# Two chunks of sequence 0 first, sequence 1's input transform spread over both, and the first weight sums split between VectorE and GpSimd

## The chip, the cores and the metric

The kernel runs on one core of one Trainium2 chip. The metric is the device time of the whole launch in microseconds. Engines are named as the profile names them: PE (matmul) with its weight loader PEld, DVE (VectorE), ACT (ScalarE), POOL (GpSimd), and SP, which here only issues DMAs. Matmul results go to PSUM, which the kernel uses as eight banks of 512 fp32 columns; everything else lies in SBUF.

## The reference

A convolution of width 3 along the sequence with 1024 input and 1024 output channels, then a batch norm from stored statistics and a SiLU:

```python
xp = jnp.pad(x, ((0, 0), (1, 1), (0, 0)))            # x: (2, 2048, 1024) bf16
y = sum(einsum('bsc,cd->bsd', xp[:, k:k + S], w[k]) for k in range(3))   # w: (3, 1024, 1024)
y = (y - mean) * (g / sqrt(var + 1e-5)) + b
return silu(y)
```

## The kernel before

**The algorithm.** The convolution is done with short polynomial products: six neighbouring output positions need eight products of transformed inputs with transformed weights, where the direct form needs eighteen. A sequence of 2048 has `NB` = 342 blocks of six positions. The input transform turns each block into eight values (`NJ` = 8) per channel, kept in SBUF as `T_sb` for both sequences. The weight transform makes, for each chunk of 128 output channels, six combinations of w0, w1, w2 (products 1 to 6); products 0 and 7 use w0 and w2 as they are.

**The input transform** (`t_jobs`, `t_job`). Rows of x are loaded in 17 overlapping windows per sequence: sixteen of up to 128 rows in the buffers `xw` (12 of them) and the first window in `xfirst`. A window is multiplied on PE by a small constant matrix, four channel tiles at a time (4 matmuls of 168 columns into two PSUM banks), and the result is copied from PSUM to `T_sb` by ACT or DVE (lines 276 and 278). I call four such matmuls with their copy a group; there are 33 groups per sequence, numbered here 0 to 32 for sequence 0 and 33 to 65 for sequence 1. A small planner with an estimated clock per engine (`clock`, `ends`, `busy`) decides, when the program is written, which of ACT and DVE copies a group. Nothing is reordered at run time: each engine works through its own list in the order written, and a PE instruction whose PSUM bank is still being copied holds up every PE instruction behind it.

**A unit** (`Unit`) is one chunk of 128 output channels (`dc`, 0 to 7) for one sequence (`bi`): eight products of 8 matmuls of 342 columns each, line 311. It owns four banks, the next unit the other four. `run` issues products 1, 3, 2, 4, 5, 6 with ACT copies of some results (`copy`, lines 322 and 324) and DVE combinations (`combine`, line 329) between them. Products 7 and 0 of a unit (`last`, `first`) and its SiLU passes (`silu_inner`, line 334) are issued during the next unit, at the places given by `place`. Product 6 is added onto product 5's bank, so it waits until ACT has copied product 5 (`pc`).

**The order before.** All 33 groups of sequence 0 run first, then 15 groups of sequence 1 (`ahead`, without products), then unit (0,0) with the last 18 groups between its matmuls (`Between`, about one group per 2.6 matmuls, in bank pairs from 4, 6 and, in the first four products, 1), and then units (0,1), (1,0), (1,1), (2,0) and so on. In unit (0,0), which has no earlier unit's products to put between its products 5 and 6, four extra calls of `between` stand there.

**The weights.** The sums of chunk 0 (`prepare_first`, written behind group 18) run on POOL: sum e0 = w0 + w2 (line 174), its two combinations u0 (line 194), and the same for e1 and e2, which need w2 and w0 times four and w1 times two. ACT makes two of these three multiples (lines 162 and 180), POOL one (line 183). Later chunks (`prepare_w`) are made two at a time, e1 and e2 as one DVE instruction each (line 176), the rest on POOL. Chunk 1 is made during unit (0,0) and the one after it.

**The loads.** SP issues them in one list: sequence 0's windows, with the three weight loads of chunk 0 behind windows number 4, 6 and 8 of the order (`W0_AT`); then sequence 1's windows, with chunk 1's weights behind numbers 5, 8 and 11 (`W1_AT`). The weights of chunks 2 and 3 follow after unit (0,0), into memory that the windows had.

Of the kernel before, what the change touches and what calls it, by code (L numbers as in the profile page):

```python
# [9 lines left out]
ALU = mybir.AluOpType  # L10
# [5 lines left out]
P = 128  # L16
R = 6
NJ = 8
W0_AT = (4, 6, 8)
W0_USE = 18  # L20
W1_AT = (5, 8, 11)
AMONG = 18
XBUFS = 12
# [3 lines left out]
def kernel(  # L27
# [24 lines left out]
    epool = ctx.enter_context(tc.tile_pool(name="epool", bufs=1))  # L52
    spool = ctx.enter_context(tc.tile_pool(name="spool", bufs=2))
    ypool = ctx.enter_context(tc.tile_pool(name="ypool", bufs=1))
    dpool = ctx.enter_context(tc.tile_pool(name="dpool", bufs=1))
# [102 lines left out]

    def double_w(dc, eng):
        t = spool.tile([P, CT, P], BF16, name="w1x2")  # L160
        if eng is nc.scalar:
            nc.scalar.mul(t, raw[dc][:, 1], 2.0)  # L162
            busy("act", CT * P)
        else:
            eng.tensor_scalar(t, raw[dc][:, 1], 2.0, 0.0, op0=ALU.mult, op1=ALU.add)
        double[dc] = t

    def even_part(dc, q, eng, by=None):

        w0, w2 = raw[dc][:, 0], raw[dc][:, 2]  # L170
        e = epool.tile([P, CT, P], FP32, name=f"e{q}")
        f, h = (w2, w0) if q == 1 else (w0, w2)
        if q == 0:
            eng.tensor_tensor(e, w0, w2, op=ALU.add)  # L174
        elif eng is nc.vector:
            eng.scalar_tensor_tensor(out=e, in0=f, scalar=4.0, in1=h, op0=ALU.mult, op1=ALU.add)  # L176
        else:
            t = spool.tile([P, CT, P], BF16, name="w1x2")
            if by is nc.scalar:
                by.mul(t, f, 4.0)  # L180
                busy("act", CT * P)
            else:
                by.tensor_scalar(t, f, 4.0, 0.0, op0=ALU.mult, op1=ALU.add)
            eng.tensor_tensor(e, t, h, op=ALU.add)
        if eng is nc.vector:
            busy("dve", CT * P)
        sums[dc, q] = e

    def transform_w(dc, q):

        o = double[dc] if q else raw[dc][:, 1]
        u = upool.tile([P, 2, CT, P], BF16, name=f"u{q}")
        for i, op in enumerate((ALU.add, ALU.subtract)):
            nc.gpsimd.tensor_tensor(u[:, i], sums[dc, q], o, op=op)  # L194
        wts[dc, q] = u

    def prepare_w(dc):

        even_part(dc, 0, nc.gpsimd)
        transform_w(dc, 0)  # L200

        def second():
            even_part(dc, 1, nc.vector)
            transform_w(dc, 1)

        def third():
            even_part(dc, 2, nc.vector)
            transform_w(dc, 2)

        act_work.append(lambda: double_w(dc, nc.scalar))  # L210
        dve_work.extend((second, third))

    def prepare_first(dc):

        even_part(dc, 0, nc.gpsimd)
        transform_w(dc, 0)
        double_w(dc, nc.scalar)
        for q, eng in ((1, nc.scalar), (2, nc.gpsimd)):
            even_part(dc, q, nc.gpsimd, eng)
            transform_w(dc, q)  # L220

# [65 lines left out]
    class Unit:  # L287
# [8 lines left out]

        def __init__(self, dc, bi, b0, lo=0, hi=NB):
            self.dc, self.bi, self.b0, self.lo, self.hi = dc, bi, b0, lo, hi
            self.bank = [ps[:, b0 + q, lo:hi] for q in range(4)]
            self.low, self.mid, self.high = (ps[:, b0 + q:b0 + q + 2, lo:hi] for q in range(3))  # L300
            self.yT = yts[bi]

# [48 lines left out]

        def run(self, between, prev, place=(5, 6), prepare=None):


            finish = {n: [] for n in range(4, 7)}
            if prev:
                finish[min(place[0], 5)].append(prev.silu_inner)
                finish[place[0]].append(lambda: prev.last(between))
                finish[place[1]].append(lambda: prev.first(between))

            def behind(n):
                for f in finish[n]:
                    f()

# [6 lines left out]
            self.product(3, 1, False, between)  # L371
            pa = self.copy(3)
            self.product(0, 3, False, between)
            pb = self.copy(0, by=4.0)
            self.product(3, 2, True, between)
            self.copy(3, dst=sd[:, 0])
            self.combine(sd[:, 1], pa, 2.0, b3, ALU.subtract)
            self.product(0, 4, True, between)
            behind(4)
# [7 lines left out]
            pc = self.copy(2)  # L387
            if not prev:
                for _ in range(4):
                    between()  # L390
            behind(5)
# [65 lines left out]
    def ahead(jobs, job_n):  # L457
        for job in jobs:
            t_job(job, job_n % 4 * 2)
            if job_n == 0:  # L460
                params()
            if job_n == 4:
                scales()
            if job_n == W0_USE:
                prepare_first(0)
            job_n += 1

    jobs0 = list(t_jobs(0))
    ahead(jobs0, 0)
    for i, wi in enumerate(order):  # L470
        load_x(1, wi)
        if i in W1_AT:
            load_w(0, W1_AT.index(i), 1)
    jobs1 = list(t_jobs(1))
    ahead(jobs1[:-AMONG], len(jobs0))

    class Between:

        n = done = 0
        jobs = jobs1[-AMONG:]  # L480

        def __call__(self):
            self.n += 1
            while self.jobs and self.done * 46 < self.n * AMONG:
                t_job(self.jobs.pop(0), (4, 6, 1)[self.done % (3 if self.n <= 4 * CT else 2)])
                self.done += 1

    between = Between()
    seq = [(dc, bi) for dc in range(DC) for bi in range(B)]
    before = prev = None  # L490
    for i, (dc, bi) in enumerate(seq[:-1]):
        unit = Unit(dc, bi, i % 2 * 4)
        unit.run(
            between, prev, (4, 4) if i >= len(seq) - 3 else (5, 6),
            1 if i == 0 else 2 if i == 2 else dc + 2 if bi == 1 and 0 < dc < DC - 2 else None,
        )
        if i == 0:
            while between.jobs:
                between()
            xwin_scope.close()  # L500
            olast = ctx.enter_context(tc.tile_pool(name="olast", bufs=2))
            wpools[1] = ctx.enter_context(tc.tile_pool(name="wpool1", bufs=1))
        if i in (0, 4, 8):
            for k in range(3):
                load_w(i // 4 + 1, k)
# [6 lines left out]
        before, prev = prev, unit  # L512
    dc, bi = seq[-1]
    h0 = Unit(dc, bi, 4, P, NB)
    h0.run(between, prev, (5, 5))
    prev.turn(olast)
    h1 = Unit(dc, bi, 0, 0, P)
    h1.run(between, h0, (5, 6))
    o = olast.tile([P, R, NK, P], BF16, name="o")
# [37 lines left out]
```

## Time and profile before

| what | value |
|---|---|
| runs | 196.32 us median of 3 (194.3 to 197.12) |
| the profiled execution | 195.83 us; span from first to last instruction 194.1 us |
| granted PE clock | 0.985 of full speed on average, 1.0 until 185 us |
| busy in the span | PE 176.8 us (91%), DVE 157.9, POOL 135.9, ACT 110.3 |
| first group / first product matmul starts | 3.90 us / 27.66 us |
| last group's matmuls start | 39.02 us to 39.84 us |

Times inside the execution count from the start of the span. A busy share is the part of a stretch in which an engine had an instruction running. A line of the timeline gives the start, the length, the engine, the line of the kernel and the tiles; in square brackets is the idle time ahead of it and what ended it. "x2" is two instructions merged into one line.

### The profile page before, as it was taken

Reading aid. Unit: us, or ns where it says so; the run is one execution under the profiler, and the core shown is the slowest. Engines: PE = TensorE matmul, PEld = TensorE weight load, DVE = VectorE, ACT = ScalarE, POOL = GpSimd, SP = SyncE. Lnnn points to the kernel's source line nnn. Section 1 sums busy time; section 2 is a strip of 40 time slices with the busy share of each in tenths; the row PEclk is TensorE's granted clock in tenths of the full one; section 3 lists DMA queues with packets and bytes.
Section 4 is the critical chain, followed back from the end, with each engine's and each line's share of the span. In section 5 each row is a group of like instructions: output and inputs, shape, how many; then the busy total and the mean of one; then the engine's idle time right before and its main releaser. Section 6 shows DMA issues by size and latency. Waiting matters only on the chain.

```text
span 194.1 us, 3673 instructions
## 1 busy us (share of the span) xinstructions
PE 176.8 (91%) x1379; PEld 125.4 (65%) x1379; DVE 157.9 (81%) x221; ACT 110.3 (57%) x185; POOL 135.9 (70%) x76
## 2 busy tenths in 40 slices
PE   1888879999999999999999999999999998989940
PEld 0876658766666666666666666666666665668920
DVE  5579866689978799988998899899889994747940
ACT  3589876774546556455546562737383572636630
POOL 5569999906796889999999999799997760000000
PEclk9999999999999999999999999999999999999985
DMA  5999998074142837597869659959649295773685
GB/s 189 310 334 306 347 330 267 8 222 107 30 91 53 179 73 159 163 217 179 163 96 202 115 117 272 209 115 193 123 111 201 50 194 99 158 156 67 151 180 120
DMA packets 89115, 32.30 MB, mean 166 GB/s; under 512 B 75721, under 2 KB 84937, under 8 KB 89097
## 3 DMA queue, kind: packets, MB, share of 16 engines
q1 hardware_dynamic: 87784, 31.75, 70.6%
q10 hardware_dynamic: 1313, 0.31, 0.7%
q8 instruction: 11, 0.18, 0.4%
q14 instruction: 7, 0.06, 0.1%
HBM read 14.82 MB, written 8.39 MB: 120 GB/s over the span
## 4 chain that ended last, share of the span: by engine, by line
PE 79%; DMA 8%; ACT 4%; DVE 2%; SPq 1%; issue 1%; ACTq 1%; DVEq 0%
PE ps L311 74%; DMA xw<-in_x_dram 6%; PE ps L265 5%; ACT yT L334 2%; DMA rows<-in_b_dram 2%; SPq L130 1%; ACT T_sb L276 1%; DVE ps L329 1%; ACTq L71 1%; ACT w1x L162 0%; ACT pc L322 0%; DVE T_sb L278 0%; DVE t L329 0%; SPq L146 0%; DVE o L413 0%
## 5 line engine op out<-in xcount | busy, mean ns | idle before, releaser
L311 PE MATMUL ps<-T_sb,u 128*128 128x342 bf16 (+2 forms) x816 | 119.8, 299 | 1.4 <-ACT pc L322 1.2
L311 PEld LDWEIGHTS <-u 128*128 128x128 bf16 x816 | 76.8, 97 | 35.3 <-issue 2.1
L194 POOL TENSOR_TENSOR u<-e,w1x 128x1024 bf16<-128x1024 f32 x32 | 70.3, 2224 | 13.8 <-DVE e L176 13.7
L311 PE MATMUL ps<-T_sb,wch 128*128 128x342 bf16 (+2 forms) x272 | 42.2, 299 | 0.0
L334 ACT ACTIVATE yT<-ps,beta,scale 128x342 bf16<-128x342 f32 (+5 forms) x51 | 34.1, 704 | 11.5 <-PE ps L311 11.5
L329 DVE SCALAR_TENSOR_TENSOR t<-ps,sd 128x684 f32<-128x684 f32 (+2 forms) x51 | 39.1, 821 | 0.6
L194 POOL TENSOR_TENSOR u<-e,wch 128x1024 bf16<-128x1024 f32 x16 | 36.6, 2310 | 1.0 <-DMA wch<-in_w_dram 0.4
L322 ACT COPY pc<-ps 128x342 f32<-128x342 f32 (+2 forms) x34 | 14.5, 427 | 33.7 <-PE ps L311 31.4
L311 PEld LDWEIGHTS <-wch 128*128 128x128 bf16 x272 | 25.6, 97 | 11.6
L265 PE MATMUL ps<-rm,xw 128*128 128x168 bf16 (+1 forms) x256 | 26.0, 248 | 6.9 <-DVE rm L100 3.9
L278 DVE CAST T_sb<-ps 128x672 bf16<-128x672 f32 x29 | 23.7, 855 | 8.1 <-PE ps L265 7.8
L276 ACT CAST T_sb<-ps 128x672 bf16<-128x672 f32 (+1 forms) x37 | 25.7, 736 | 7.8 <-PE ps L265 7.7
L176 DVE SCALAR_TENSOR_TENSOR e<-wch 128x1024 f32<-128x1024 bf16 x14 | 29.2, 2084 | 0.0
L265 PEld LDWEIGHTS <-xw 128*128 128x128 bf16 (+1 forms) x256 | 21.2, 104 | 11.8 <-DMA xw<-in_x_dram 6.0
L329 DVE SCALAR_TENSOR_TENSOR ps<-ps,t 128x684 f32<-128x684 f32 (+2 forms) x34 | 28.3, 832 | 0.6
L329 DVE SCALAR_TENSOR_TENSOR ps<-ps,pc 128x342 f32<-128x342 f32 (+2 forms) x34 | 16.9, 497 | 11.5 <-PE ps L311 8.5
L174 POOL TENSOR_TENSOR e<-wch 128x1024 f32<-128x1024 bf16 x8 | 19.0, 2374 | 3.4 <-DMA wch<-in_w_dram 3.4
L334 ACT ACTIVATE yT<-t,beta,scale 128x684 bf16<-128x684 f32 (+2 forms) x17 | 15.7, 925 | 0.0
L329 DVE SCALAR_TENSOR_TENSOR t<-ps,t 128x684 f32<-128x684 f32 (+2 forms) x17 | 13.9, 818 | 0.0
L329 DVE SCALAR_TENSOR_TENSOR sd<-pc,ps 128x342 f32<-128x342 f32 (+2 forms) x17 | 8.3, 486 | 6.8 <-ACT sd L322 6.8
L322 ACT COPY sd<-ps 128x342 f32<-128x342 f32 (+2 forms) x17 | 7.3, 428 | 10.4 <-PE ps L311 10.4
L324 ACT ACTIVATE pc<-ps 128x342 f32<-128x342 f32 (+2 forms) x17 | 7.5, 441 | 9.4 <-PE ps L311 5.9
(38 smaller groups left out, 33.3 us busy)
## 6 DMA issues: line engine op xcount, KB each, us to landing
xw<-in_x_dram SPq DMA_DIRECT2D x30, 256.0 KB
out_dram<-o SPq DMA_DIRECT2D x30, 192.0 KB
wch<-in_w_dram SPq DMA_DIRECT2D x9, 512.0 KB
out_dram<-o SPq DMA_DIRECT2D x15, 120.0 KB
wch<-in_w_dram SPq DMA_DIRECT2D x6, 256.0 KB
xfirst<-in_x_dram SPq DMA_DIRECT2D x2, 224.0 KB
o<-yT SPq DMA_TRANSPOSE x15
out_dram<-o SPq DMA_DIRECT2D x15, 7.5 KB
```

The costliest lines, as they stand in the source:

```text
L71: nc.scalar.dma_start(out=rows[q * DC:(q + 1) * DC, :], in_=ap.rearrange("(dc p) -> dc p", p=P))
L174: eng.tensor_tensor(e, w0, w2, op=ALU.add)
L176: eng.scalar_tensor_tensor(out=e, in0=f, scalar=4.0, in1=h, op0=ALU.mult, op1=ALU.add)
L194: nc.gpsimd.tensor_tensor(u[:, i], sums[dc, q], o, op=op)
L265: nc.tensor.matmul(v[:, c * nb // nct, c % (nct // nb)], lhsT=xw[0:rows, (c0 + c) * P:(c0 + c + 1) * P], rhs=rm[0:rows, :, 0:n], start=Tru ...
L276: nc.scalar.copy(dst, src)
L278: nc.vector.tensor_copy(dst, src)
L311: nc.tensor.matmul(self.bank[q], lhsT=lhsT, rhs=T_sb[:, ct, j, nsl], start=not add and ct == 0, stop=ct == CT - 1, skip_group_check=add,)
L322: nc.scalar.copy(dst, self.bank[q])
L324: nc.scalar.mul(dst, self.bank[q], by)
L329: nc.vector.scalar_tensor_tensor(out=out, in0=in0, scalar=scalar, in1=in1, op0=ALU.mult, op1=op1)
L334: nc.scalar.activation(self.yT[:, rows, self.lo:self.hi], src, ACT.Silu, bias=beta[:, dc:dc + 1], scale=scale[:, dc:dc + 1])
```

## The change

- The units run in the order (0,0), (1,0), (0,1), (1,1), and from chunk 2 on as before. The two halves of a staging buffer `yT` are now taken in turn by unit number.
- Only sequence 0's 33 groups run ahead. Sequence 1's 33 groups go between the matmuls of the first two units by a plan (`AMONG`): 19 in the first 32 matmuls of unit (0,0) (banks 4, 6, 1), 6 in its last 16; 4 in the first 32 matmuls of unit (1,0) (bank 5) and 4 by its 62nd (bank 1), counting the matmuls of products 7 and 0 of unit (0,0), which lie in unit (1,0) at place (4, 5). The four extra calls of `between` are gone.
- Chunk 0's weights: the three multiples, e0 and both combinations u0 move to DVE, written behind groups 10 to 16 of the transform; e1, u1, e2, u2 stay on POOL. ACT makes none.
- Chunk 1's weights are all made early: `second_w`, behind the second product of unit (0,0), puts nine sums on POOL and three multiples on DVE. Before, DVE made two sums and ACT one multiple of it.
- Chunk 0's weight loads stand behind windows 2, 3 and 4; chunk 1's ahead of all of sequence 1's windows. The loads for chunks 2 and 3 follow after unit (1,0).

```diff
-W0_AT = (4, 6, 8)
-W0_USE = 18
-W1_AT = (5, 8, 11)
-AMONG = 18
+W0_AT = (2, 3, 4)
+AMONG = ((32, 19, (4, 6, 1)), (48, 25, (4, 6))), ((32, 29, (5,)), (62, 33, (1,)))
...
-    def prepare_first(dc):
-
-        even_part(dc, 0, nc.gpsimd)
-        transform_w(dc, 0)
-        double_w(dc, nc.scalar)
-        for q, eng in ((1, nc.scalar), (2, nc.gpsimd)):
-            even_part(dc, q, nc.gpsimd, eng)
-            transform_w(dc, q)
+    def both(dc, q):
+        even_part(dc, q, nc.gpsimd)
+        transform_w(dc, q)
+
+    v = nc.vector
+    first_w = {
+        10: lambda: times(0, 2, 4, v), 11: lambda: even_part(0, 0, v), 12: lambda: times(0, 1, 2, v),
+        13: lambda: transform_w(0, 0, v, (0,)), 14: lambda: transform_w(0, 0, v, (1,)),
+        15: lambda: both(0, 1), 16: lambda: times(0, 0, 4, v), 17: lambda: both(0, 2),
+    }
+
+    def second_w():
+
+        even_part(1, 0, nc.gpsimd)
+        transform_w(1, 0)
+        for k, by in ((2, 4), (1, 2), (0, 4)):
+            times(1, k, by, v)
+        both(1, 1)
+        both(1, 2)
...
-            if not prev:
-                for _ in range(4):
-                    between()
...
-            if job_n == W0_USE:
-                prepare_first(0)
+            if job_n in first_w:
+                first_w[job_n]()
...
+    for k in (0, 2, 1):
+        load_w(0, k, 1)
+    for wi in order:
         load_x(1, wi)
-        if i in W1_AT:
-            load_w(0, W1_AT.index(i), 1)
-    jobs1 = list(t_jobs(1))
-    ahead(jobs1[:-AMONG], len(jobs0))
...
-    seq = [(dc, bi) for dc in range(DC) for bi in range(B)]
+    seq = [(dc, bi) for bi in range(B) for dc in range(2)]
+    seq += [(dc, bi) for dc in range(2, DC) for bi in range(B)]
...
+        place = (4, 5) if i == 1 else (4, 4) if i >= len(seq) - 3 else (5, 6)
         unit.run(
-            between, prev, (4, 4) if i >= len(seq) - 3 else (5, 6),
-            1 if i == 0 else 2 if i == 2 else dc + 2 if bi == 1 and 0 < dc < DC - 2 else None,
+            between, prev.rest(between, *place) if prev else [(2, second_w)],
+            dc + 2 if bi == 1 and dc < DC - 2 else None,
         )
```

`times(dc, k, by, eng)` makes a multiple of w[k] (`tensor_scalar` on DVE, bf16 to bf16, 1024 elements per partition), `even_part` a sum e, and `transform_w` the two combinations of e with w1 or twice w1. The planner counts 420 ns for a multiple on DVE and 1.2 us for a sum.

## The prediction

> **What bounds the kernel now.** I read the table of stretches first, to see where PE is short of work, then the timeline of PE, then that of DVE, of POOL and of ACT around the change. In the table the columns after the length are the busy times of PE, PEld, DVE, ACT and POOL, then granted clock, DMA share and GB/s.
>
> ```profile
> 10.00:20.00 10.00, 8.50 (x99) 7.07 (x97) 9.11 (x12) 9.32 (x15) 8.43 (x4) 1.00 1.08 324
> 20.00:28.00 8.00, 6.42 (x69) 4.73 (x67) 6.84 (x9) 6.38 (x10) 7.74 (x5) 1.00 1.11 337
> 28.00:40.00 12.00, 11.73 (x117) 9.06 (x117) 7.81 (x12) 9.06 (x16) 10.22 (x5) 1.00 0.48 142
> 40.00:100.00 60.00, 59.99 (x414) 39.99 (x413) 53.98 (x66) 33.20 (x56) 49.98 (x22) 1.00 0.63 138
> ```
>
> From 40 us on PE is full: whatever the first 40 us lose or gain moves the end by as much. From 10 to 20 us DVE and ACT, which copy the groups, are nine tenths full; from 20 to 28 us the windows of sequence 1 arrive too slowly (1.11 of the DMA engines). PE's timeline gives the marks:
>
> ```profile
> 26.39 1.14 PE L265 MATMUL ps<-rm,xw 128*128 128x168 bf16 x12 [0.86 <-DMA xw<-in_x_dram]
> 27.66 0.30 PE L311 MATMUL ps<-T_sb,u 128*128 128x342 bf16 x1
> ...
> 39.84 7.29 PE L311 MATMUL ps<-T_sb,u 128*128 128x342 bf16 x48
> ```
>
> The first product starts at 27.66 us. The 48 product matmuls from 39.84 us take until 46.97 us, 0.148 us each; the next eight take 1.17 us, so I use **0.146 us a matmul**. A group between products costs 0.29 us of PE (28.09 to 28.38 us, four matmuls). The mark I compare by is "all 66 groups and 112 product matmuls issued", which is the end of the second unit in either order. Counting the timeline on from 46.97 us (88 matmuls) before reaches it at 50.46 us.
>
> **What can be gained.** Starting the first product right behind sequence 0's groups moves 15 groups, 15 x 0.29 = 4.35 us, behind it. From the first product the stretch needs 112 x 0.146 + 33 x 0.29 = 16.35 + 9.57 = 25.9 us, if nothing waits. So the change wins only if that product starts before 50.46 - 25.9 = **24.6 us**, less every new wait.
>
> **What the first weights cost on DVE.** The multiples of w on DVE are not in the trace. The nearest row for length is a one-input bf16 DVE copy of 1024 elements (681 ns); the ends are 0.425 us (the same copy, 512 elements) and 1.22 us (line 176, two inputs, alone). I take 0.68. The sums e0 and u0 are two-input instructions on 1024 elements with everything in SBUF, like line 176; these rows show what such a one meets:
>
> ```profile
> 44.17 1.22 DVE L176 SCALAR_TENSOR_TENSOR e<-wch 128x1024 f32<-128x1024 bf16 x1
> ...
> 113.71 5.20 POOL L194 TENSOR_TENSOR u<-e,w1x 128x1024 bf16<-128x1024 f32 x2
> ...
> 113.94 2.98 DVE L176 SCALAR_TENSOR_TENSOR e<-wch 128x1024 f32<-128x1024 bf16 x1
> ```
>
> With POOL idle it takes 1.22 us. At 113.94 us POOL is in the first of two sums; DVE's takes 2.98 us, and POOL's second, issued at 115.80 us, takes 3.11 instead of 2.13 us. The waits fit one reading: only one of the two runs at a time, and the one that waits goes ahead of the next instruction of the one that ran. Instructions with an input in PSUM (the 684-column combinations, 863 ns on average) show no such wait. Whether the multiples, one input but all in SBUF, wait is open: I let them wait like line 176, the only DVE instruction before that lies in SBUF alone, and keep "not at all" as the other end (rival B).
>
> The Trainium skill ("SBUF — State Buffer", section "Who interferes with whom") says the same more strongly: a DVE instruction with two SBUF inputs excludes a GpSimd one that reads SBUF, and so does a one-input `tensor_scalar` in a two-port mode; the second to come blocks fully. No row here shows the one-input case; by the page the multiples wait and B falls. For the length, "VectorE: DVE Perf Modes" (section "The perf-mode tier table") gives 693 ns for 2048 bf16 elements, about 0.42 us for 1024 by my estimate; sum A would be some 1.6 us smaller.
>
> **Step 1, the transform of sequence 0.** Six instructions come to DVE (3 x 0.68 + 3 x 1.22 = 5.7 us) and two leave ACT (2.1 us, lines 162 and 180); the written order gives ACT groups 12 to 18 in a row and DVE groups 19, 21, 23, 26, 28, 30 and 32 behind its sums. DVE's chain with alternation: group 9 copied by 10.8 us (DVE's fifth copy; its fourth ran 9.91 to 10.77 before, and window 4 now stands behind two weight loads); w2 times four to 11.5; POOL's e1 to 13.65; DVE's e0, waiting, to 14.85; w1 times two to 15.5; first u0 to 16.7; POOL's first u1 to 18.85; second u0 to 20.05; POOL's second u1 to 22.2; w0 times four to 22.9. Then seven copies, six at 0.83 (thirteen take 10.74 us at 11.49 us) and a small one: 5.5 us. The first product needs all of them: **28.4 us**. PE can't run past this: group 23 wants the banks of group 19.
>
> The loads hide here: windows 5 to 9 come up to 1.6 us later at first (two weight loads of 0.26 MB at 324 GB/s), in step again by group 18, by which as many loads are out in both orders. Chunk 1's three halves now stand in SP's queue ahead of sequence 1's windows; sequence 0 and six halves are 5.8 MB, in by about 20.3 us at the page's rates, so windows are there by 23 us.
>
> **Step 2, units (0,0) and (1,0).** Four waits on PE, none of them in the trace of before:
> - DVE reaches chunk 1's three multiples after 16 matmuls and 10 groups, 28.4 + 5.2 + 0.9 for its copy = 34.5 us. POOL still has its sums queued (from 22.9 us: three for chunk 0, three for chunk 1, 12.8 us). With alternation: 3 x 0.68 + 2 x 2.13 = 6.3 us, to 40.8; the copy of group 46 behind them to 41.7. PE wants that bank for group 49 at 28.4 + 27 x 0.146 + 16 x 0.29 = 37.0 us: **4.7 us**. Without waits for POOL 0.4 us.
> - Product 6 of unit (0,0) waits for ACT's copy of product 5, which the extra groups covered. Uncovered it costs 0.59 us near the end; three group copies stand ahead of it on ACT (0.65 us each where they run back to back): 1.1 us.
>
> ```profile
> 161.53 5.96 PE L311 MATMUL ps<-T_sb,u 128*128 128x342 bf16 x40 [0.59 <-ACT pc L322]
> ```
>
> - Group 58 and a combination wait for copies of the groups just before: 0.9 us.
> - Group 62 writes banks that unit (0,0)'s SiLU still reads, one matmul behind its issue. ACT's two passes take 959 + 911 ns behind group 61's copy: 1.6 us. All 33 groups' loads and POOL's queue are not late here: POOL is through chunk 1 by about 50 us, product 5 of unit (1,0) comes after 56 us.
>
> Bounds for the last three, 3.6 us together: nothing, if ACT and DVE run ahead, to 5 us, if ACT (eight groups, four copies, four SiLU passes in unit (1,0), some 11 us of its 11.7) falls behind.
>
> **Moved at no cost.** The loads of chunks 2 and 3 go out one unit later; before, they went out at 38.96 us and were first read at 55.09 us, so 16 us of cover shrink to about 5; if it is gone, PE loses up to 1 us at unit (2,0). ACT loses chunk 1's multiple, DVE two sums of it (1.2 and 1.9 us), both beside PE's work. Unit order and staging buffers change no count.
>
> **Sum A**: 28.4 + 25.9 + 4.7 + 3.6 = 62.6, against 50.5: 12 us later, 195.83 + 12 = **207.8 us**. The profiled execution is 0.5 us under the median of the runs, less than their spread.
>
> **Rivals.**
> - **B, half of the waits**: the multiples don't wait for POOL, or DVE, once on, isn't overtaken by POOL. First: w0's multiple ends at 20.7, first product 26.2, waits 0.4 + 3.6: 56.1. Second: second u0 ends at 17.9, first product 24.1, and the multiples wait for one POOL sum (2.5 + 3.6): 56.1. 201.4 us. For it: no row shows one-input instructions in SBUF, nor DVE's next one against a waiting POOL. Against: in the rows above POOL's own next instruction stood ready and was overtaken.
> - **C, no waits for POOL**, only those on ACT: 22.9 + 25.9 + 4.0 = 52.8, 198.1 us. Against it: line 176's mean of 2084 ns.
> - **D, faster**: DVE's sums fit beside ACT's seven copies (C's chain, 22.9 us), and the waits of step 2 are covered, as ACT and DVE alternate within each 0.53 us that PE gives a group: 48.8, 1.7 us early, **194.1 us**. It decides as soon as the first product and the waits add to less than 24.6 us. For it: PE idles 1.6 of the 8 us from 20 us before. Were the copies also quicker, 20.6 us (where sequence 0's last group ran before) is the earliest start: 191.8.
>
> **How the numbers follow.** A 0.42 (204 to 211), B 0.30 (199.5 to 203), C 0.13 (197 to 199.5), D 0.10 (191.8 to 196), later than 211 0.05. The range 198 to 211 leaves out D, the last, and a little of C. 2% of the time, 3.9 us, is about what a measurement of this kernel can tell from no change: slower by more is A, what lies beyond it and most of B, 0.73; within it the rest of B, C and most of D, 0.22; faster 0.05.
>
> **What would show it.** In the profile after: e0 or the u0 sums on DVE above 2 us, each beside a POOL sum; the first product at 28 us (A), 24 to 26 (B), 23 (C, D); three multiples in unit (0,0) with over 2 us each from start to start, and PE idle for DVE's copy behind them; PE idle for ACT's `pc` at the sixth product and for a SiLU at group 62. A first product before 24 us with no PE wait over 1 us behind it would make the prediction wrong.

## The result and the profile after

The changed kernel takes **205.19 us** (median of 4 runs, 204.24 to 205.47); the kernel before took 195.93 us beside it (4 runs, 194.3 to 197.12). The ratio is **1.047, 95% interval 1.038 to 1.056**: slower. The forecast was 207.8 us with the range 198 to 211. The ratios, here and below, leave out two slow runs, over 1.5% above the fastest of their kernel (206.91 us of sums_first and 204.18 us of balanced_loads), while the medians contain them. The profiled execution took 204.24 us, its span 202.5 us; 8.4 us more than before's 194.1.

The same table of stretches, now of the changed kernel (length; busy times of PE, PEld, DVE, ACT and POOL; granted clock; DMA share; GB/s):

```profile
10.00:20.00 10.00, 5.36 (x55) 3.88 (x53) 9.19 (x9) 7.21 (x11) 6.96 (x3) 0.95 1.13 329
20.00:28.00 8.00, 5.21 (x47) 4.80 (x47) 6.73 (x8) 3.59 (x5) 7.56 (x5) 0.63 0.97 286
28.00:40.00 12.00, 10.27 (x108) 8.45 (x107) 10.34 (x13) 8.48 (x14) 11.48 (x6) 1.00 0.54 184
40.00:100.00 60.00, 57.40 (x423) 39.10 (x423) 46.35 (x59) 36.23 (x61) 40.68 (x19) 1.00 0.54 119
```

PE has 5.36 us of work from 10 to 20 us where it had 8.50, and 57.40 instead of 59.99 from 40 to 100 us. The granted clock fell to 0.63 from 20 to 28 us; it was 1.00 before. PE's timeline of the changed kernel:

```profile
22.30 4.22 PE L275 MATMUL ps<-rm,xw 128*128 128x168 bf16 x36 [4.82 <-DVE T_sb L288]
...
27.78 0.30 PE L321 MATMUL ps<-T_sb,u 128*128 128x342 bf16 x1 [0.49 <-ACT T_sb L286]
...
38.05 0.45 PE L275 MATMUL ps<-rm,xw 128*128 128x168 bf16 x4 [1.56 <-DVE T_sb L288]
...
43.09 0.30 PE L321 MATMUL ps<-T_sb,u 128*128 128x342 bf16 x1 [0.86 <-ACT pc L332]
...
45.97 0.45 PE L275 MATMUL ps<-rm,xw 128*128 128x168 bf16 x4 [0.39 <-ACT T_sb L286]
...
53.25 0.45 PE L275 MATMUL ps<-rm,xw 128*128 128x168 bf16 x4 [1.31 <-ACT yT L344]
...
57.87 4.37 PE L321 MATMUL ps<-T_sb,u 128*128 128x342 bf16 x29
```

PE stands idle for 4.82 us before 22.30 us, for a group that waits for DVE's copy of group 19. The first product starts at 27.78 us, not earlier than before (27.66), though 15 groups fewer lie ahead of it. Then come 1.56 us for DVE and 0.86, 0.39 and 1.31 us for ACT. Eight of the last line's matmuls complete the mark, "66 groups and 112 product matmuls issued": 57.87 + 8 x 0.146 = **59.04 us**, 8.6 us later than the 50.46 of before. What follows the mark took the same time (202.5 - 59.0 = 143.5, before 194.1 - 50.5 = 143.6), so the whole loss lies in front of it. In DVE's timeline, the instructions that the change put there:

```profile
10.98 0.42 DVE L165 TENSOR_SCALAR w2x<-wch 128x1024 bf16<-128x1024 bf16 x1
...
12.78 1.90 DVE L176 TENSOR_TENSOR e<-wch 128x1024 f32<-128x1024 bf16 x1
14.61 0.41 DVE L165 TENSOR_SCALAR w1x<-wch 128x1024 bf16<-128x1024 bf16 x1
14.94 4.28 DVE L192 TENSOR_TENSOR u<-e,wch 128x1024 bf16<-128x1024 f32 x2
19.14 2.34 DVE L165 TENSOR_SCALAR w0x<-wch 128x1024 bf16<-128x1024 bf16 x1
...
34.04 0.59 DVE L165 TENSOR_SCALAR w2x<-wch 128x1024 bf16<-128x1024 bf16 x1
34.55 0.41 DVE L165 TENSOR_SCALAR w1x<-wch 128x1024 bf16<-128x1024 bf16 x1
34.89 2.35 DVE L165 TENSOR_SCALAR w0x<-wch 128x1024 bf16<-128x1024 bf16 x1
```

and, in POOL's, those beside them:

```profile
15.16 6.03 POOL L192 TENSOR_TENSOR u<-e,w1x 128x1024 bf16<-128x1024 f32 x2 [1.56 <-DVE w1x L165]
...
34.71 2.23 POOL L180 TENSOR_TENSOR e<-w2x,wch 128x1024 f32<-128x1024 bf16 x1 [0.36 <-DVE w2x L165]
```

A multiple takes 0.41 to 0.42 us when POOL is idle (w1 times two at 14.61 us, w2 times four at 10.98). The two sums u0, 1.2 us each alone, take 4.28 us beside POOL's pair u1, which takes 6.03 instead of the 4.2 of a pair alone. w0 times four, a one-input instruction, takes 2.34 us: it waits out the second of POOL's sums, which ends at 21.19 us. Between 10.98 and 21.4 us DVE copies one group; PE, out of banks, stands behind it.

### The profile page after: what moved, and what is told of

It reads as the page before. It is cut to its first block, busy times and chain, and to the rows that moved or that the text cites. A ratio compares the mean times of both kernels' runs of the same rounds, so it can differ in the third digit from the quotient of the medians.

```text
span 202.5 us, 3686 instructions
## 1 busy us (share of the span) xinstructions
PE 177.3 (88%) x1379; PEld 126.7 (63%) x1379; DVE 160.5 (79%) x221; ACT 112.5 (56%) x189; POOL 135.6 (67%) x74
## 4 chain that ended last, share of the span: by engine, by line
PE 74%; DVE 7%; DMA 5%; ACT 5%; issue 3%; SPq 1%; ACTq 0%; DVEq 0%
PE ps L321 68%; DMA xw<-in_x_dram 5%; PE ps L275 5%; ACT yT L344 3%; DVE T_sb L288 2%; ACT T_sb L286 2%; DVE w0x L165 1%; DVE e L176 1%; DVE ps L339 1%; SPq L129 1%; DVE u L192 1%; ACT pc L332 1%; DVE sd L339 1%; SPq L145 0%; DVE w1x L165 0%
## 5 line engine op out<-in xcount | busy, mean ns | idle before, releaser
L321 PE MATMUL ps<-T_sb,u 128*128 128x342 bf16 (+2 forms) x816 | 121.8, 299 | 2.7 <-ACT pc L332 2.0
L192 POOL TENSOR_TENSOR u<-e,w1x 128x1024 bf16<-128x1024 f32 x32 | 72.2, 2279 | 7.5 <-DVE e L178 4.4
L275 PE MATMUL ps<-rm,xw 128*128 128x168 bf16 (+1 forms) x256 | 28.7, 256 | 14.4 <-DVE T_sb L288 6.4
L286 ACT CAST T_sb<-ps 128x672 bf16<-128x672 f32 (+1 forms) x44 | 31.1, 747 | 17.7 <-PE ps L275 17.3
L275 PEld LDWEIGHTS <-xw 128*128 128x128 bf16 (+1 forms) x256 | 23.1, 107 | 21.5 <-issue 13.4
L192 POOL TENSOR_TENSOR u<-e,wch 128x1024 bf16<-128x1024 f32 x14 | 33.3, 2402 | 0.6
L176 POOL TENSOR_TENSOR e<-wch 128x1024 f32<-128x1024 bf16 x7 | 16.8, 2404 | 16.1 <-DMA wch<-in_w_dram 16.1
L178 DVE SCALAR_TENSOR_TENSOR e<-wch 128x1024 f32<-128x1024 bf16 x12 | 24.7, 2059 | 0.0
L288 DVE CAST T_sb<-ps 128x672 bf16<-128x672 f32 (+1 forms) x22 | 18.3, 843 | 7.2 <-PE ps L275 6.9
```

The lines of the kernel that those rows point to most:

```text
L192: eng.tensor_tensor(wts[dc, q][:, i], sums[dc, q], o, op=op)
L275: nc.tensor.matmul(v[:, c * nb // nct, c % (nct // nb)], lhsT=xw[0:rows, (c0 + c) * P:(c0 + c + 1) * P], rhs=rm[0:rows, :, 0:n], start=Tru ...
L286: nc.scalar.copy(dst, src)
L288: nc.vector.tensor_copy(dst, src)
L321: nc.tensor.matmul(self.bank[q], lhsT=lhsT, rhs=T_sb[:, ct, j, nsl], start=not add and ct == 0, stop=ct == CT - 1, skip_group_check=add,)
```

## The experiments

The mark explains every run that follows: the span less the mark lies between 143.2 and 143.7 us in all of them. All numbers of this table but the last two columns are read from the PE timelines; "waits" is PE's idle time between the first product and the mark (waits of 0.15 us and more). What remains is the mark less the first product, the waits and the work itself: 25.9 us with 33 groups behind the first product, 112 x 0.146 + 18 x 0.29 = 21.6 us with the 18 of the old order. About 1 us of remains, or a little more, is in all of them, before too, and I call it the short gaps: idle times under 0.15 us, and the last matmul ahead of each pause, which takes 0.30 us to its end where in a row the next one starts 0.146 us behind it. What goes beyond 2 us is, above all, matmuls at half clock. A mark is read from one execution, and the runs of one kernel lie 1.0 us (pe_kept_busy) to 3.7 us (sums_first) apart; a difference of 1 us between two marks says little.

| kernel | first product | waits | remains | mark | median us | ratio (95%) |
|---|---|---|---|---|---|---|
| before | 27.66 | 0 | 1.2 | 50.46 | | |
| changed | 27.78 | 4.3 | 1.0 | 59.04 | 205.19 | 1.047 (1.038-1.056) |
| sums_first | 21.69 | 9.4 | 4.7 | 61.7 | 204.50 | 1.044 (1.038-1.051) |
| second_on_pool | 29.29 | 3.4 | 1.0 | 59.5 | 204.09 | 1.044 (1.039-1.048) |
| sums_first_second_on_pool | 22.69 | 5.5 | 1.7 | 55.8 | 200.84 | 1.026 (1.020-1.031) |
| before_first_on_dve | 32.71 | 0.3 | 1.1 | 55.7 | 201.81 | 1.033 (1.028-1.037) |
| waits_only | 28.46 | 2.3 | 1.6 | 58.3 | 203.41 | 1.041 (1.037-1.046) |
| pe_kept_busy | 33.88 | 4.2 | 1.0 | 65.0 | 209.37 | 1.073 (1.070-1.076) |
| pe_kept_busy_2 | 27.18 | 5.4 | 2.5 | 61.0 | 205.31 | 1.047 (1.043-1.051) |
| order_only | 21.47 | 4.7 | 2.6 | 54.7 | 199.88 | 1.022 (1.017-1.027) |
| balanced | 21.43 | 5.3 | 4.7 | 57.3 | 202.60 | 1.037 (1.032-1.041) |
| order_loads_waits | 22.02 | 4.3 | 3.6 | 55.8 | 201.28 | 1.028 (1.024-1.032) |
| balanced_loads | 22.23 | 5.2 | 3.3 | 56.6 | 201.16 | 1.027 (1.023-1.031) |
| order_mended | 20.91 | 2.6 | 1.9 | 51.3 | 198.12 | 1.015 (1.011-1.019) |

**Theory at the start:** DVE and POOL exclude each other here, and the exclusions hold up DVE's copies, first in the transform (4.8 us), then in unit (0,0) (1.8 us); the rest is waits for ACT that the old order covered. **Rivals:** the added instructions are simply too much for DVE, exclusion or not; or the 33 groups among two units are what costs, whoever makes the weights.

### sums_first: the same instructions on DVE, before POOL has work

```diff
-10: times(0, 2, 4, v), 11: even_part(0, 0, v), 12: times(0, 1, 2, v),
-13: transform_w(0, 0, v, (0,)), 14: transform_w(0, 0, v, (1,)),
-15: both(0, 1), 16: times(0, 0, 4, v), 17: both(0, 2),
+10: even_part(0, 0, v), 11: transform_w(0, 0, v, (0,)), 12: transform_w(0, 0, v, (1,)),
+13: times(0, 1, 2, v), 14: times(0, 0, 4, v), 15: times(0, 2, 4, v),
+16: both(0, 1), 17: both(0, 2),
```

> The changed kernel with chunk 0's work on DVE in another order: e0 and both u0 first, then the multiples of w1, w0 and, last, w2, which POOL's e1 waits for; so POOL reads nothing while DVE's sums run. The planner now gives DVE groups 17, 19, 21, 24, 26, 28, 30 and 32. Theory (DVE and POOL wait for each other): e0 and u0 take 1.22 us each, DVE is through by 16 us in place of 21.4, the first product starts near 22.5 us in place of 27.8, with no gap of several us on PE before it and full granted clock from 20 to 28 us. DVE then meets chunk 1's multiples while POOL still has sums that need none of them, so PE waits some 5 us there in place of 1.8: about 2 us less in all, 203 us. Rival 1 (the load of six more instructions on DVE, not waiting, is the cost): sums still 2 us each, first product at 27.8, 205 us. Rival 2 (33 groups among two units are the cost): first product early, the gain lost in PE waits for ACT.

The DVE timeline of this kernel:

```profile
11.35 1.22 DVE L176 TENSOR_TENSOR e<-wch 128x1024 f32<-128x1024 bf16 x1
12.60 2.36 DVE L192 TENSOR_TENSOR u<-e,wch 128x1024 bf16<-128x1024 f32 x2
14.88 0.42 DVE L165 TENSOR_SCALAR w1x<-wch 128x1024 bf16<-128x1024 bf16 x1
...
31.25 2.16 DVE L165 TENSOR_SCALAR w2x<-wch 128x1024 bf16<-128x1024 bf16 x1
33.34 2.34 DVE L165 TENSOR_SCALAR w1x<-wch 128x1024 bf16<-128x1024 bf16 x1
35.60 2.33 DVE L165 TENSOR_SCALAR w0x<-wch 128x1024 bf16<-128x1024 bf16 x1
```

POOL's first sum needs w2 times four, the last of DVE's six, so DVE works alone: 1.22, 2.36 and three times 0.42 us, 4.6 us in place of 10.5 (one copy among them), and the first product starts at 21.69 us, 6.1 us earlier. That the load of DVE as such is too much falls. The gain is then lost again in unit (0,0). POOL's sums of both chunks now stand in one unbroken queue beside DVE's three multiples of chunk 1, and each multiple waits for a whole sum: 2.16, 2.34, 2.33 us. PE meets that as one wait in its timeline:

```profile
38.75 0.72 PE L276 MATMUL ps<-rm,xw 128*128 128x168 bf16 x4 [5.04 <-DVE T_sb L289]
```

(The profiled execution of this kernel was the longest of its four, 206.91 us; the others took 203.20 to 205.55. So its mark is late for them by up to 3.7 us, and no trace shows which of its waits they have. Besides the 5.04 us there is one of 1.79 us for a window, at 23.79 us, and with each of the two goes a time at half clock.)

### second_on_pool and sums_first_second_on_pool: chunk 1's multiples on POOL itself

```diff
 for k, by in ((2, 4), (1, 2), (0, 4)):
-    times(1, k, by, v)
+    times(1, k, by, nc.gpsimd)
+    clock["dve"] += 420.0
```

> The changed kernel with chunk 1's three multiples on POOL in place of DVE, everything else in its place (the planner's clock is still advanced by the 420 ns). Theory: DVE's copy of group 46 is no longer late, PE's 1.6 + 0.2 us of waiting for DVE in unit (0,0) go, POOL's three multiples of about 1.05 us each are covered since u1 is needed 3 us later than it is ready: 203.4 us, 1.8 us less. Rival (these waits are covered by others behind them, as ACT is the later one): PE waits longer for ACT at product 6 and group 62, no change, 205 us.

> Both edits together. Theory: first product near 22.5 us, no PE wait for DVE in unit (0,0); now POOL is late, since its 18 sums and multiples begin only at 16 us: PE waits about 3 us for the first u1 of chunk 1 in unit (1,0). 201.5 us. If POOL were not the next bound: 198 us. Rival 2 (the groups among two units are the cost): 203 us or more, with the PE waits at ACT.

With the first alone, PE's wait for DVE in unit (0,0) falls from 1.56 + 0.20 to 0.62 + 0.17 us. What is left has nothing to do with POOL: DVE's combination `sd` waits for ACT's copy, and DVE's copies behind it are late, as PE's and DVE's timelines show:

```profile
39.78 0.45 PE L276 MATMUL ps<-rm,xw 128*128 128x168 bf16 x4 [0.62 <-DVE T_sb L289]
...
38.45 0.51 DVE L340 SCALAR_TENSOR_TENSOR sd<-pc,ps 128x342 f32<-128x342 f32 x1 [0.78 <-ACT sd L333]
```

So of the changed kernel's 1.76 us about 1.0 is, by this comparison, the multiples' own. The time falls by less than the runs can tell (204.09); in its profiled execution the transform ended 1.5 us later for other reasons (e0 took 2.61 us). Both edits together give 200.84 us. Two of the waits left in PE's timeline:

```profile
23.63 0.46 PE L277 MATMUL ps<-rm,xw 128*128 128x168 bf16 x4 [0.63 <-DMA xw<-in_x_dram]
...
44.04 0.32 PE L323 MATMUL ps<-T_sb,u 128*128 128x342 bf16 x1 [1.15 <-POOL u L192]
```

POOL, with the multiples on top of its sums, becomes late itself (1.15 us at 44.04), and the first window of sequence 1 is late (0.63 us) now that the first product comes early.

### before_first_on_dve: the weights step alone, in the order of before

```diff
-W0_AT = (4, 6, 8)
+W0_AT = (2, 3, 4)
...
-            if job_n == W0_USE:
-                prepare_first(0)
+            if job_n in first_w:
+                first_w[job_n]()
```

> The kernel before with one part of the change: chunk 0's multiples, e0 and u0 on DVE in the changed kernel's order, with the weight loads behind windows 2, 3 and 4; order of units, 15 groups ahead and 18 in unit (0,0) as before. Theory: DVE's sums wait for POOL as in the changed kernel, PE stands still near 17 to 22 us, the first product comes near 32.3 us in place of 27.7 and the last group near 44.5 in place of 39.5: 200.6 us, 4.7 us more than before. Rival 2 (the groups among two units are the cost): within 1 us of before.

It costs 5.2 us at the mark (55.70 against 50.46) and 3.3% in time. In PE's timeline there is the wait of the changed kernel again, 4.29 us where that had 4.82:

```profile
22.45 3.85 PE L268 MATMUL ps<-rm,xw 128*128 128x168 bf16 x36 [4.29 <-DVE T_sb L281]
```

So the stall belongs to the weights step (with its earlier loads), not to the order.

### order_only: the order without the weights step

The weights of both chunks are made as before (ACT, POOL, and later DVE); the order of the units, the 33 groups among two of them and the order of the loads are the changed kernel's.

```diff
+    def first_old():
+        both(0, 0)
+        times(0, 1, 2, nc.scalar)
+        times(0, 2, 4, nc.scalar)
+        both(0, 1)
+        times(0, 0, 4, nc.gpsimd)
+        both(0, 2)
+
+    first_w = {18: first_old}
...
+    def second_a():
+        both(1, 0)
+        times(1, 1, 2, nc.scalar)
+    def second_b():
+        even_part(1, 1, v)
+        transform_w(1, 1)
+    def second_c():
+        even_part(1, 2, v)
+        transform_w(1, 2)
...
-            between, prev.rest(between, *place) if prev else [(2, second_w)],
+            between, prev.rest(between, *place) if prev else [(1, second_a), (4, second_b), (6, second_c)],
```

> The changed kernel with the weights of both chunks made on the engines of the kernel before: those of chunk 0 on GpSimd and ScalarE behind group 18, those of chunk 1 on ScalarE, VectorE and GpSimd in three steps in unit (0,0). Left of the change are the order of the units, the transform of sequence 2 among the first two units and the order of the loads. Theory (the loss is VectorE's and GpSimd's excluding each other, and the order itself is worth a little): no stall of 4.8 us, the first product at about 22 us in place of 27.8; the waits for ScalarE stay (2.6 us), one wait of up to 1.2 us for GpSimd and one of 1 to 2 us for a load come in; mark of 66 groups and 112 product matmuls at about 53 us against 59.0, so about 199 us, ratio 1.015. Rival (33 groups among two units are what costs, whoever makes the weights): 203 or more.

199.88 us, ratio 1.022: the mark is 54.7, not 53, and still 4.2 us behind before's, so neither reading was the whole of it. The first product is 6.2 us early, as expected. Of this 4.35 us are only moved (15 groups, 0.29 us each). What is left, 1.8 us, is more than spent on waits of 4.65 us and on something that I had not counted, seen in PE's timeline and in a table of stretches of 2 us (length, PE, then clock, DMA share and GB/s):

```profile
21.47 0.31 PE L337 MATMUL ps<-T_sb,u 128*128 128x342 bf16 x1 [0.84 <-ACT T_sb L302]
23.52 0.46 PE L291 MATMUL ps<-rm,xw 128*128 128x168 bf16 x4 [1.74 <-DMA xw<-in_x_dram]
```

```profile
22.00:24.00 2.00, 0.48 (x6) 1.00 1.03 324
24.00:26.00 2.00, 2.00 (x17) 0.68 0.97 329
26.00:28.00 2.00, 2.00 (x14) 0.50 1.03 375
```

PE reaches sequence 1's first window before it is there, waits 1.74 us, and from 24.7 to 28.1 us runs at half clock. Of those 3.4 us half is lost, 1.7 us: 21.47 + 25.9 + 4.65 + 1.7 = 53.7, and 1 us of short gaps as everywhere.

### waits_only: the waits for ACT

```diff
-AMONG = ((32, 19, (4, 6, 1)), (48, 25, (4, 6))), ((32, 29, (5,)), (62, 33, (1,)))
+AMONG = ((32, 19, (4, 6, 1)), (40, 21, (4, 6)), (44, 23, (4, 6)), (52, 25, (4, 6))), ((32, 29, (5,)), (40, 29, ()), (62, 33, (1,)))
...
             pc = self.copy(2)
+            if self.dc == 0 and self.bi == 0:
+                for _ in range(4):
+                    between()
```

> The changed kernel with three edits that touch nothing but what TensorE does ahead of ScalarE's copies: four more groups are issued behind the copy of product 6 in unit (0,0), and the last groups among units (0,0) and (1,1) are dealt out in smaller steps ahead of the copies that they stand behind. Theory (the waits for ScalarE in these two units are time on the path): the wait for the copy of product 6 falls from 0.86 us to about 0.4, that of the last groups behind the SiLU from 1.31 to about 0.4, so about 1.2 us less: 204.0 us, ratio 0.994. Rival (ScalarE itself is full there, and the waits only move to the next matmul): no change, 205.2.

The waits in PE's timeline that were 0.86, 0.39 and 1.31 us:

```profile
43.79 0.45 PE L275 MATMUL ps<-rm,xw 128*128 128x168 bf16 x4 [0.32 <-ACT T_sb L286]
...
45.93 0.45 PE L275 MATMUL ps<-rm,xw 128*128 128x168 bf16 x4 [0.24 <-ACT T_sb L286]
...
53.21 0.45 PE L275 MATMUL ps<-rm,xw 128*128 128x168 bf16 x4 [0.15 <-ACT yT L344]
```

From the first product to the mark it takes 58.27 - 28.46 = 29.8 us instead of 31.26, 1.4 us less; the median is 203.41 us. The theory holds; the two intervals of the ratio overlap, so the size rests on the traces.

### balanced: both steps mended at once

The order of instructions on DVE is that of sums_first, the three edits are those of waits_only, and chunk 1 is made by the three functions shown with order_only, a little earlier:

```diff
-            between, prev.rest(between, *place) if prev else [(2, second_w)],
+            between, prev.rest(between, *place) if prev else [(1, second_a), (2, second_b), (4, second_c)],
```

> The order of the units and loads as changed, chunk 0's sums of weights on VectorE first and its multiples behind them (as in sums_first), chunk 1's weights spread as before over GpSimd, ScalarE and VectorE but begun in the first half of unit (0,0), and the three edits of waits_only. Theory: first product at about 22 us as in sums_first (21.69), no wait of 5 us in unit (0,0), waits for ScalarE 1.4 us in place of 2.6, waits for loads and GpSimd up to 2.5: mark at about 52 to 53 us, so 198 us, ratio 1.01. If it is under 1.0 the order of the units is worth something by itself; rival (VectorE's two sums of chunk 1 wait for GpSimd's as they did in the transform stage, and TensorE for them): 201 or more.

A miss: 202.60 us, and the rival's side. PE waits 2.94 us for sequence 1's window until 24.68 and its clock is at half from 23.3 to 30.1 us (5.4 us of work at half clock, some 2.7 lost). Of DVE's two sums of chunk 1 the first did not wait (1.21 us at 32.80 us; POOL's pair beside it took 5.28 us in place of 4.2); the second took 2.65 us beside one and held PE up for 1.08 us at 44.96 us. PE's timeline, then DVE's:

```profile
24.68 0.74 PE L282 MATMUL ps<-rm,xw 128*128 128x168 bf16 x4 [2.94 <-DMA xw<-in_x_dram]
...
38.60 2.65 DVE L178 SCALAR_TENSOR_TENSOR e<-wch 128x1024 f32<-128x1024 bf16 x1
```

Its first product, 21.43 us, is where order_only's is: making the first weights on VectorE, even in its better order, starts nothing earlier than POOL and ACT do.

### order_loads_waits, balanced_loads and order_mended: taking the load's wait away

```diff
-    for k in (0, 2, 1):
-        load_w(0, k, 1)
-    for wi in order:
+    for i, wi in enumerate(order):
         load_x(1, wi)
+        if i in (3, 5, 7):
+            load_w(0, (0, 2, 1)[(i - 3) // 2], 1)
```

> order_only, with chunk 1's three loads issued behind the fourth, sixth and eighth window of sequence 1 in place of ahead of them all, and with the three edits of waits_only. Theory (what kept order_only above before is a list of waits, each of which can be taken away by itself): from order_only's mark of 54.67 us the wait for a load (1.74) goes, the halved clock that follows it (2.65 us left over in the sum 21.47 + 25.9 + 4.65 = 52.0) goes with it, and 1.4 us of waits for ScalarE go: mark about 48.9 us, against 50.46 before, 194.2 us, ratio 0.992. Rival (GpSimd now waits for chunk 1's loads, and TensorE for GpSimd): mark above 51, ratio over 1.0.

> balanced, with chunk 1's three loads issued behind the fourth, sixth and eighth window of sequence 1. Theory: from balanced's mark of 57.29 us the wait for a load (2.94) goes, and with it the halved clock that followed it (4.7 us left over in the sum 21.43 + 25.9 + 5.28 = 52.6); VectorE's two waits for GpSimd's sums of chunk 1 stay (1.9 us of TensorE's time): mark about 50, 195.2 us, ratio 1.00, and 1 us more than order_loads_waits, so that making chunk 0's weights on VectorE is worth nothing by itself. Rival (the first weights on VectorE free GpSimd early enough to pay): at least 1 us less than order_loads_waits.

Both missed (201.28 and 201.16 us). The wait for the window at 23.5 us was gone, but a new one came, as ACT's timeline of order_loads_waits and then PE's tell:

```profile
28.58 1.06 ACT L162 ACTIVATE w1x<-wch 128x1024 bf16<-128x1024 bf16 x1 [3.24 <-DMA wch<-in_w_dram]
```

```profile
30.34 0.72 PE L291 MATMUL ps<-rm,xw 128*128 128x168 bf16 x4 [2.56 <-DMA xw<-in_x_dram]
```

ACT's multiple of chunk 1 is written ahead of its copies and now waits 3.24 us for its load; PE stands behind the copies and then runs at half clock until 33.4 us. (The timeline names a window's load at 30.34 us; that it is ACT that was late follows from ACT's next copies, which begin at 29.54 us. In balanced_loads the trace names ACT's copy itself, for a stall of 3.50 us.) It was not POOL, as the rival had it. So what the weights on VectorE are worth by themselves can't be read from this pair; 22.0 and 22.2 us for the first product show no gain. The last kernel moves that one instruction:

```diff
     def second_a():
         both(1, 0)
-        times(1, 1, 2, nc.scalar)
...
-    [(1, second_a), (4, second_b), (6, second_c)]
+    [(1, second_a), (3, lambda: times(1, 1, 2, nc.scalar)), (4, second_b), (6, second_c)]
```

> order_loads_waits with ScalarE's multiple of chunk 1 issued two products later: there it stood in front of ScalarE's copies and waited for its load until 28.58 us, and TensorE for the copies behind it (2.56 us without a matmul, and the clock at 0.50 afterwards). Theory (that stall was the new one; the order of the units is worth nothing even with its stalls taken away, since TensorE saves 27.66 - 22.0 = 5.6 us before the first product but carries 11 more groups, 3.2 us, and about 1.7 us of small waits and 1 us between them behind it): mark 22.0 + 25.9 + 1.7 + 1.0 = 50.6 us against 50.46 before, 196.0 us, ratio 1.00. Rival (the multiple or GpSimd's sums of chunk 1 are late elsewhere): mark over 52, ratio 1.01 or more.

198.12 us, ratio 1.015 (1.011 to 1.019): the nearest that this order came. The profiled execution is the fastest of its six runs (196.86 us) and is close to the theory: mark 51.3 against 50.6, clock 1.00 from 10 to 100 us, no wait above 1.05 us behind the first product (for POOL's `u` at 40.15 us). The ratio, though, is the rival's (1.01 or more). (The expectation speaks of 11 groups that are moved behind the first product; it is 15, 4.35 us, and its sum did not use the number.) The six runs reach 199.37 us, and no trace shows what the longer ones have more of; that is open. No version beat before.

### pe_kept_busy and pe_kept_busy_2: is it PE's idling that halves the clock, and does it cost time?

```diff
+            if job_n == 23:
+                for _ in range(80):
+                    nc.tensor.matmul(ps[:, 1, 384:512], lhsT=ident, rhs=ident, start=True, stop=True)
```

(in the first of the two, bank 7 instead of 1; the products of these matmuls are not used.)

> The changed kernel with 80 matmuls of 128 columns of the identity into an unused part of the accumulators, issued ahead of the group at which TensorE stood idle for 4.82 us; their results are used by nothing. By 0.070 us for 168 columns at full clock they take about 80 x 0.053 = 4.3 us, so they fit into the idle time. Theory (the lower granted clock behind the idle time, 0.63 from 20 to 28 us with 0.117 us for a matmul of a group, follows from TensorE's standing idle): the clock stays near 1.0 in that stretch, the 36 matmuls behind the wait take about 2.5 us in place of 4.22, and the first product starts up to 1.7 us earlier; VectorE's seven copies, 5.5 us from the end of its last multiple at 21.5, hold it at 27.0, so about 0.8 us less: 204.4. Rival (the clock has another cause, or the copies are the bound throughout): no change, 205.2.

> As pe_kept_busy, but the 80 matmuls go to the bank of group 20, which ScalarE has copied by about 17.6 us, and so do not wait for VectorE's copy of group 19; they can run in the 4.82 us in which TensorE stood idle. Theory (the halved clock, 0.50 from 18.9 to 25.75 us in the changed kernel's trace and from 20.95 to 27.65 in pe_kept_busy's, is set off by TensorE's standing idle): with the idle time filled the clock stays near 1.0 up to 28 us, the 36 matmuls of groups behind the wait take about 2.5 us in place of 4.22, and the first product starts 0.8 us earlier (VectorE's copies then hold it): 204.4 against the changed kernel's 205.2. Rival (the clock has another cause, the loads for instance): clock and time as in the changed kernel.

The first failed as an experiment: bank 7 was the one that DVE had yet to copy, so the 80 matmuls waited out the stall (5.50 us) and came on top, 6.90 us, most of it at half clock; 209.37 us. In the second they fill it. Its PE timeline and two rows of its table of stretches:

```profile
17.90 4.63 PE L475 MATMUL ps<-ident 128*128 128x128 bf16 x80 [0.17 <-ACT T_sb L286]
22.99 2.94 PE L275 MATMUL ps<-rm,xw 128*128 128x168 bf16 x36 [0.47 <-DVE T_sb L288]
...
27.18 0.30 PE L321 MATMUL ps<-T_sb,u 128*128 128x342 bf16 x1 [0.45 <-ACT T_sb L286]
...
38.76 0.45 PE L275 MATMUL ps<-rm,xw 128*128 128x168 bf16 x4 [2.85 <-DVE T_sb L288]
```

```profile
20.00:28.00 8.00, 7.03 (x100) 6.11 (x98) 7.42 (x8) 3.55 (x6) 7.56 (x4) 1.00 1.02 307
...
40.00:42.00 2.00, 2.00 (x12) 1.52 (x11) 1.38 (x2) 0.77 (x1) 2.00 (x2) 0.50 0.00 0
```

With the stall filled the clock stays at 1.00 from 20 to 28 us, so its fall there does come from PE's idling. From the end of the stall to the first product it is 27.18 - 22.99 = 4.2 us in place of 5.5: the halved clock had cost 1.3 us there. In the time it can't be found (205.31 us): in the profiled execution POOL reached chunk 1's e1 0.7 us later than in the changed kernel's (35.42 us), PE came 0.6 us earlier, and its wait for DVE grew from 1.56 to 2.85 us, since w2 times four now came early in a POOL sum (1.89 us in place of 0.59). Behind that wait the clock fell after all, from 39.4 to 42.9 us, which cost some 1.6 us. (This execution, 206.1 us, was the longest of six.) The cause of the clock's fall is settled; what it is worth in the changed kernel is 1.3 us or less of 8.6.

## Why the prediction was right, and where it was off

**The chain on DVE** (28.4 us): the first product came at 27.78 us. The sums and multiples beside POOL went as described: e0 behind POOL's e1 (1.90 us), the two u0 alternating with POOL's u1 (4.28 us), and w0 times four waiting too, which was the open point between the forecast and rival B. The multiples were taken at 0.68 us, from the row of the copy; they take 0.41 to 0.42 alone; that row (line 413, `o<-ps`) reads PSUM, the multiples read SBUF.

That the chain came within 0.6 us of the sum is in part luck, for two larger misses cancel. w0 times four ended at 21.48 us, 1.4 us before the 22.9 of the sum. Then the seven copies, 5.5 us in the sum, took 6.8 us, from 21.40 to 28.19, since DVE had to wait 0.89 and 0.26 us for groups that PE made at half clock. The sum has no term for the clock and gives no reason for leaving it out. Where it stayed at 1.00, the copies took what the sum says. DVE's timeline of the changed kernel, then of pe_kept_busy_2:

```profile
24.81 0.86 DVE L288 CAST T_sb<-ps 128x672 bf16<-128x672 f32 x1 [0.89 <-PE ps L275]
...
22.09 5.54 DVE L288 CAST T_sb<-ps 128x672 bf16<-128x672 f32 x7
```

The Trainium skill ("SBUF — State Buffer", section "Who interferes with whom") had said that a one-input `tensor_scalar` can take the port shared with GpSimd and then blocks fully. The runs agree: 2.34 us beside a POOL sum, 0.41 without. The estimate of 0.42 us from "VectorE: DVE Perf Modes" (section "The perf-mode tier table") was nearer than the row that I chose.

**DVE's multiples of chunk 1** (4.7 us): this is the term that was mis-sized, measured 1.56 + 0.20 = **1.76 us**. The step let two sums of POOL run between the three multiples. But POOL's next sum, e1, reads w2 times four, the first of the three, so POOL itself had to wait (0.36 us at 34.71 us) and w1 times two slipped through in 0.41 us; only w0 times four waited a whole sum (2.35 us), so the three took 3.2 us from start to end and not 6.3. And 0.79 us of the 1.76 stay without any multiple on DVE (second_on_pool), where the step had 0.4. How long an instruction waits depends on whether the other engine's next one is free to run. In sums_first, where POOL's queue was free to run, all three waited and PE lost 5.04 us: the mechanism was right, the state of POOL's queue was not looked up.

**The three waits for ACT** (3.6 us): 0.86 + 0.39 + 1.31 = 2.56 us, at the places named, `pc` at product 6, group 58, group 62 behind the SiLU. They were priced 0.2, 0.5 and 0.3 us too high. waits_only confirms that they are time on the path.

**The sum**: 27.78 + 25.9 + 1.76 + 2.56 = 58.0, and 1.0 us of short gaps, for which the prediction had no term, make 59.0; forecast 62.6. (The mark of before, 50.46, has 1.2 us of such gaps in it, so the forecast counted them on one side only.) Of the 3.6 us between them 2.9 are chunk 1's multiples, 1.0 ACT, 0.6 the first product, less that 1.0. With the terms as measured the sum gives 195.83 + 8.6 = 204.4 us, at the lower end of A's band.

**The costs put at nothing**: the loads of chunks 2 and 3, one unit later, made POOL idle for 14.6 us (to 62.35 us) and PE not at all. Sequence 1's windows, "there by 23 us", were hidden only because the first product was late: where it starts at 21.4 us, the first window's group cannot start before 23.5 (order_only) or 24.7 us (balanced).

**Rivals C and D** counted with a chain of 22.9 us, C with the small waits as its only ones (4.0 us), D with none. sums_first_second_on_pool had that first product (22.69 us) and took 200.84 us, not 198.1: waits for windows (0.63 and 0.39 us) and for POOL (1.15 us) came on top of those for ACT. D's conditions held in none of the runs; order_mended has a first product at 20.91 us and still ends 0.9 us behind before: of the 6.75 us of earlier start, 4.35 go to the 15 groups behind it, 2.6 to waits and 0.7 to more short gaps.

**So where the 8.6 us come from**, by two one-step kernels: the order with its groups and loads costs 4.2 us (order_only, 54.67), the weights step another 4.4 us on top (59.04); alone in the old order it costs 5.2. By the spread of the runs each of these shares is good to about 1 us.

## What to carry to other kernels

Before work is moved to VectorE beside a busy GpSimd, list for each moved instruction what GpSimd's queue can run at that moment: an instruction that lies in SBUF alone waits for a whole one of GpSimd's, and the copies behind it wait with it. If it must be there, put it where GpSimd has nothing it could start. And a start that is pulled forward is worth only what the next resource allows (here the windows' loads): ask what comes late at the new time, not at the old one.

## What the runs showed of the hardware

**Two engines, one at a time, in turns.** Who waits goes ahead of the next instruction of the other engine: two sums on each side, 2.4 and 4.2 us alone, took 4.28 and 6.03 us beside each other, and three multiples beside an unbroken POOL queue took one sum each.

**The granted clock falls by half, in steps of time.** The changed kernel's table in stretches of 2 us (length, PE, then clock, DMA share and GB/s):

```profile
18.00:20.00 2.00, 0.00 (x0) 0.77 1.34 225
20.00:22.00 2.00, 0.00 (x0) 0.50 1.15 258
...
24.00:26.00 2.00, 2.00 (x18) 0.53 0.95 298
26.00:28.00 2.00, 1.51 (x22) 1.00 0.93 323
```

Idle from 17.5 us, the clock is at 0.50 from about 19.0 to 25.9 us, 6.8 us, long after PE has work again. In balanced the half clock lasted from 23.3 to 30.1 us, 6.8 us; in order_only from 24.7 to 28.1 and in order_loads_waits from 30.0 to 33.4, 3.4 us; in second_on_pool from 18.5 to 28.7, 10.2 us: one, two or three times the same length. The fall can come after the work has resumed (order_only, 1.2 us after). What it costs is half of the time that PE works in it, where PE is the bound: about 1.7 us in order_only and 2.7 in balanced. A wait of 1.74 us thus cost PE as much again afterwards. The length of one wait does not decide it: in before_first_on_dve the clock was at half from 11.6 to 15.0 us after two waits of 0.88 us each for windows, 0.75 us of work apart, while the changed kernel's wait of 1.56 us at 38.05 us left it at 1.00.

The Trainium skill ("TensorE: Matmul & The Clock Gate", section "Part 1: The HAM clock gate") describes free-running windows of about 3.4 us and half rate after an idle one. The half rate and the steps agree; a whole idle window was not needed here: order_only's longest gap was 1.74 us, with 0.84 us and one matmul just before it, and before_first_on_dve's gaps were shorter still.
